# Pooled attention with a SoLU feed-forward on one core: the second product of a tile one slot later

## The chip, the cores and the metric

The kernel runs on one core of one Trainium2 chip. The metric is device time in microseconds, the median of several executions. TensorE appears as PE (matmuls) and PEld (weight loads), VectorE as DVE, ScalarE as ACT, GpSimd as POOL, and the queue from which SyncE issues DMAs as SP or SPq.

## What is computed

Four batches of 12288 queries with 128 channels attend to 768 pooled keys each, and the result goes through a feed-forward block with a softmax-weighted activation and a layer norm:

```
kv_flat = mean over 4x4 patches of kv, reshaped, @ w_sr      # keys = values, 768 x 128
s = (q @ k.T) / sqrt(128);  a = softmax(s);  x = a @ v
h = x @ w_in                                                  # 1024 wide
u = h * softmax(h)
ln = (u - mean(u)) / sqrt(var(u) + 1e-6) * g_ln
out = ln @ w_out                                              # 128 wide
```

## The kernel before

There are 384 tiles (`NT`) of 128 tokens, 96 per batch, four to a group (`GT`), 96 groups (`NG`). Products are made in split precision: an operand is a 16-bit high part plus a 16-bit low part, and a product is three matmul passes. The order of all instructions is written out by hand (`manual_schedule`): each engine works through its instructions in exactly the order in which the source emits them, and the only other order is that of the waits between engines for data and for buffers.

The main loop (line 1056) runs over 384 slots. In one slot the engines work on several tiles, each at another stage. Counted from the slot of its scores, a tile passes these stages; a name with a line number is the instruction as the trace shows it:

- Slot 0: DVE takes the negated row maximum of the scores (`nm`, L575), ACT the exponential (`s`, L576) and its 16-bit high part (`phl`, L578), DVE the low part (`phl`, L586), and SP transposes both by DMA (`pT`, L589). The scores themselves (PE, `s`, L555) were made one slot earlier.
- Slots 2 to 6 of the last tile of a group, for the whole group: PE makes `xa` (L622), ACT and DVE split it (`xh` L629, `xl` L634), DVE takes a reciprocal (`rz`, L657).
- Slot 9: PE makes `h` (L675). Slot 10 (`LH`): DVE takes its maximum (`junkd`, L683), ACT the exponential (`e`, L699).
- Slot 11: DVE makes `u` (L713), POOL its high part (L730) and low part (L737) in `uhl`, ACT the sum of squares (`junk`, L778), and `hidden_turn` (line 750) issues the DMA that transposes `uhl` into `uT` (L752). `uT` has 4 buffers (line 746).
- Slot 13 (`LO`, line 44): `final_pe` (line 788) makes `o`, the second product of the block: 24 matmuls of 128 columns that read `uT` (L803).
- Per group: `final_scale` (ACT, `f`, L813) and `final_root` (POOL, L820 and L821) make the norm factor; `final_out` (line 823) is called at `slot - LO - 1` of the last tile of a group: it multiplies on DVE (`ob`, L826) and issues the store to HBM on SP (L835).

`final_out` runs once per group, so it falls in a fixed one of every four slots. With the slot number taken modulo four, the extra work per group lies so: in slots 3 ACT has `f` and SP the load of queries (`qf`, L503); in slots 0 ACT has `xh`, and SP, where keys of the next batch are due, a load of 384 KB (`kv`, L229); in slots 1 DVE has `xl` early and `rz` late, ACT `rz` (L662) and the high part of the next queries (`qh`, L533). In the kernel before, `ob` and its store are in slots 1, behind `rz`, too. Slots 2 have nothing extra.

PSUM holds three 2-bank buffers that scores and `h` share (`ps_r`), one bank for `xa` and one for `o` (`ps_o`). So `h` of a slot waits for the DVE `phl` of that slot to release a buffer, and the first `o` of a group waits for `ob` of the group before it.

Keys of batch 0 are made before the loop and used in a wider format, which makes its slots longer on PE. Those of batches 1 to 3 are loaded and added up in slots up to 62, 64 to 156 and 160 to 252 (one load in 6 slots) and turned into `kh`, `kl` and `vhl` in slots 69 to 92 of the batch before (165 to 188 and 261 to 284 for batches 2 and 3).

After the loop a list of calls (`tail`, line 1160) finishes the last ten tiles. In it `("o", -4)` is the second product of tile `NT - LH - 4`, and so on. The last slot of the loop makes no `o` (line 1107).

Of the kernel before, what the change touches and what calls it, by code (L numbers as in the profile page):

```python
# [40 lines left out]
XSP = 5  # L41
NORM = 6
LH = 10
LO = 13
FSC = 12
QSP = 1

# [20 lines left out]
def kernel(  # L68
# [429 lines left out]
    def q_load(g):  # L498
        if g >= NG or g % QL:
            return  # L500
        b, gb = divmod(g, GPB)
        t = dmt.tile([P, QL * 512], F32, tag="qf", name=f"qf_{g}", bufs=3)
        nc.sync.dma_start(t, qT[b, :, gb * 512 : (gb + QL) * 512])  # L503
        state["qf", g // QL] = t
# [121 lines left out]
    def values_out(g):  # L626
        b = g * GT // TPB
        xh = grp.tile([P, 512], F16, tag="xh", name=f"xh_{g}")
        nc.scalar.activation(xh, state["xa", g], AF.Copy, scale=state["sv", b][:, 1:2])  # L629
        state["x", g] = (xh, grp.tile([P, 512], F16, tag="xl", name=f"xl_{g}"))  # L630
# [12 lines left out]
    def values_norm(g):  # L643
        b = g * GT // TPB
        zz = grp.tile([P, 2, GT], F32, tag="zz", name=f"zz_{g}", bufs=2)
        rz = grp.tile([P, 3, GT], F32, tag="rz", name=f"rz_{g}", bufs=3)
        z, bb = state.pop(("z", g)), state["bb", b]
        for k in range(2):
            nc.gpsimd.tensor_scalar(
                zz[:, k, :], z, 1e-9, bb[:, 3 + k : 4 + k], op0=ALU.add, op1=ALU.mult  # L650
            )
        state["zz", g] = (zz, rz)
# [383 lines left out]
    def at(t, fn, *args):  # L1036
        if 0 <= t < NT:
            fn(t, *args)

    def at_last(t, fn, *args):  # L1040

        if 0 <= t < NT and t % GT == GT - 1:
            fn(t // GT, *args)
# [12 lines left out]
    for slot in range(NT):  # L1056
# [50 lines left out]
        if slot < NT - 1:  # L1107
            at(slot - LO, final_pe)
        if late:
            values(av, qtr, 1)  # L1110
        at(i - 1, hidden_turn)
        if slot % GT == GT - 1:
            q_load(slot // GT + 3)
        at_last(slot - LO - 1, final_out)
        at_last(slot - XSP, values_out)
# [44 lines left out]
    def tail(steps):  # L1160
        for name, *ts in steps:
            fn = {
                "h": hidden_pe, "o": final_pe, "max": hidden_max, "e": hidden_exp,
                "u": hidden_u, "hl": split, "sq": hidden_var,
                "t": hidden_turn_pe, "th": hidden_turned_high, "tl": hidden_turned_low,
            }[name]
            for t in ts:
                fn(NT - LH + t)
# [1 line left out]
    xa(G - 1, 3)  # L1170
    values_norm(G - 1)
    values_norm(G)
    tail([("h", 1), ("u", -1)])
    values_out(G - 1)
    tail([("max", 0), ("e", 0), ("hl", -1)])
    scale(G - 1)
# [129 lines left out]
```

## Time and profile before

| | |
|---|---|
| median of 3 runs | 1850.34 us (1846.69 to 1851.47) |
| the profiled execution | 1846.07 us, span 1844.2 us |
| busy: PE, PEld | 1819.9 us (99%), 1187.9 us (64%) |
| busy: ACT, DVE, POOL | 1781.8 (97%), 1768.6 (96%), 1684.9 (91%) |
| PE, ACT, DVE busy in 560 to 700 us | 136.43, 135.49, 134.61 of 140 |
| PE, ACT, DVE busy in 1500 to 1640 us | 140.00, 139.02, 137.89 of 140 |
| DMA busy share, bytes per time | 1.19 and 235 GB/s in 560 to 700 us, 1.18 and 227 GB/s in 1500 to 1640 us |
| TensorE clock granted | 0.999 of the upper level |
| DMA issues | `pT` x384, 4.1 us to landing; `uT` x378, 4.5 us |

Shares of busy time are averages over stretches with different limits. PE's row counts a matmul until its modelled end, which lies after the start of the next one, so a PE at 100% may still start its matmuls late; waits and start-to-start times say more. The share of the DMA engines counts the packets of 16 engines and can be over 1 since an engine has more than one packet under way.

### The profile page before, as it was taken

Reading aid. Unit: us, or ns where it says so; the run is one execution under the profiler, and the core shown is the slowest. Engines: PE = TensorE matmul, PEld = TensorE weight load, DVE = VectorE, ACT = ScalarE, POOL = GpSimd, SP = SyncE. Lnnn points to the kernel's source line nnn. Section 1 sums busy time; section 2 is a strip of 40 time slices with the busy share of each in tenths; the row PEclk is TensorE's granted clock in tenths of the full one; section 3 lists DMA queues with packets and bytes.
Section 4 is the critical chain, followed back from the end, with each engine's and each line's share of the span. In section 5 each row is a group of like instructions: output and inputs, shape, how many; then the busy total and the mean of one; then the engine's idle time right before and its main releaser. Section 6 shows DMA issues by size and latency. Waiting matters only on the chain.

```text
span 1844.2 us, 42743 instructions
## 1 busy us (share of the span) xinstructions
PE 1819.9 (99%) x15723; PEld 1187.9 (64%) x15723; DVE 1768.6 (96%) x2635; ACT 1781.8 (97%) x3124; POOL 1684.9 (91%) x1466
## 2 busy tenths in 40 slices
PE   8999999999999999999999999999999999999998
PEld 5567777777666666666666666666666666666666
DVE  6999999999999999999999999999999999999997
ACT  5999999999999999999999999999999999999997
POOL 5899999899999999989999999998998989898987
PEclk9999999999999999999999999999999999999999
DMA  8999999999999999999999999999999999999998
GB/s 301 211 221 241 233 242 238 237 235 239 240 240 231 239 238 246 246 235 235 236 238 243 240 242 241 240 242 226 222 233 233 232 229 229 228 230 238 227 211 176
DMA packets 1440027, 432.80 MB, mean 235 GB/s; under 512 B 1404608, under 2 KB 1408832, under 8 KB 1439552
## 3 DMA queue, kind: packets, MB, share of 16 engines
q1 hardware_dynamic: 1439664, 429.97, 115.3%
q8 instruction: 126, 2.06, 0.5%
q14 instruction: 93, 0.76, 0.1%
q10 hardware_dynamic: 144, 0.00, 0.0%
HBM read 52.50 MB, written 25.17 MB: 42 GB/s over the span
## 4 chain that ended last, share of the span: by engine, by line
ACT 44%; PE 32%; POOL 9%; issue 7%; DMA 3%; DVE 3%; SPq 0%; POOLq 0%; DVEq 0%
ACT e L699 12%; ACT junk L778 12%; PE o L803 9%; ACT phl L578 9%; PE h L675 8%; PE s L555 7%; ACT s L576 7%; PE xa L622 7%; POOL uhl L737 4%; ACT qh L533 2%; POOL uhl L730 2%; DMA uT<-uhl 2%; DMA kv<-in_kv_dram 1%; DVE junkd L683 1%; ACT xh L629 1%
## 5 line engine op out<-in xcount | busy, mean ns | idle before, releaser
L737 POOL TENSOR_TENSOR uhl<-u,uhl 128x1024 f16<-128x1024 f32 x382 | 814.9, 2134 | 31.6
L803 PEld LDWEIGHTS <-uT 128*128 128x128 f16 x9072 | 537.0, 98 | 97.6 <-DMA uT<-uhl 11.8
L803 PE MATMUL o<-wch,uT 128*128 128x128 f16 x6048 | 568.2, 219 | 5.9 <-DMA uT<-uhl 5.8
L803 PE MATMUL o<-wcl,uT 128*128 128x128 f16 x3024 | 525.9, 219 | 0.0
L713 DVE SCALAR_TENSOR_TENSOR u<-h,rz,e 128x1024 f32<-128x1024 f32 x384 | 491.0, 1279 | 29.7 <-ACT e L699 22.8
L683 DVE TENSOR_SCALAR_CACHE_REDUCE junkd<-h,rz 128x1024 bf16<-128x1024 f32 x384 | 490.5, 1277 | 1.5 <-PE h L675 1.1
L622 PE MATMUL xa<-pT,vhl 128*128 128x512 f16 x1728 | 468.9, 380 | 0.0
L699 ACT ACTIVATE e<-h,nm,rz 128x1024 f32<-128x1024 f32 x384 | 458.5, 1194 | 3.0 <-DVE junkd L683 3.0
L730 POOL TENSOR_SCALAR uhl<-u 128x1024 f16<-128x1024 f32 x379 | 397.0, 1047 | 66.3 <-DVE u L713 57.8
L778 ACT ACTIVATE junk<-u,su 128x1024 bf16<-128x1024 f32 x384 | 437.4, 1139 | 0.1
L575 DVE TENSOR_REDUCE nm<-s 128x1 f32<-128x768 f32 x384 | 363.8, 947 | 15.5 <-PE s L555 14.6
L586 DVE SCALAR_TENSOR_TENSOR phl<-s,phl 128x768 f16<-128x768 f32 x384 | 365.6, 952 | 5.0 <-ACT phl L578 4.9
L576 ACT ACTIVATE s<-s,nm 128x768 f32<-128x768 f32 x384 | 335.0, 872 | 6.3 <-DVE nm L575 5.9
L578 ACT ACTIVATE phl<-s 128x768 f16<-128x768 f32 x384 | 311.5, 811 | 12.1
L675 PEld LDWEIGHTS <-xh 128*128 128x128 f16 x1536 | 140.4, 97 | 197.5 <-DVE phl L586 39.1
L622 PEld LDWEIGHTS <-vhl 128*128 128x128 f16 x1728 | 162.1, 98 | 140.8 <-issue 13.1
L675 PE MATMUL h<-w_in_h,xh 128*128 128x512 f16 x768 | 229.1, 380 | 2.9 <-DVE rz L657 1.8
L675 PE MATMUL h<-w_in_h,xl 128*128 128x512 f16 x768 | 228.4, 379 | 0.0
L675 PE MATMUL h<-w_in_l,xh 128*128 128x512 f16 x768 | 228.4, 379 | 0.0
L555 PEld LDWEIGHTS <-qh 128*128 128x128 f16 x1152 | 108.0, 98 | 56.5 <-issue 0.6
L555 PE MATMUL s<-kh,qh 128*128 128x384 f16 x576 | 140.5, 325 | 0.4 <-DVE u L713 0.3
L555 PE MATMUL s<-kh,ql 128*128 128x384 f16 x576 | 140.7, 326 | 0.0
(150 smaller groups left out, 1856.1 us busy)
## 6 DMA issues: line engine op xcount, KB each, us to landing
kv<-in_kv_dram SPq DMA_DIRECT2D x64, 384.0 KB, 4.5
qf<-in_q_dram SPq DMA_DIRECT2D x96, 256.0 KB, 3.3
out_dram<-ob SPq DMA_DIRECT2D x96, 256.0 KB, 2.7
pT<-phl SPq DMA_TRANSPOSE x384, 4.1
uT<-uhl SPq DMA_TRANSPOSE x378, 4.5
raw_in<-in_moe_w_in_dram SPq DMA_DIRECT2D x1, 1024.0 KB, 5.2
raw_out<-in_moe_w_out_dram SPq DMA_DIRECT2D x1, 1024.0 KB, 9.6
room<-uhl SPq DMA_TRANSPOSE x5, 3.7
```

Of the source, the lines that this page charges most:

```text
L555: nc.tensor.matmul(s[:, half, :384], lh[:, ts], rh[:, half * 384 : (half + 1) * 384], start=n == 0, stop=n == 2,)
L576: nc.scalar.activation(s, s, AF.Exp, bias=nm, accum_out=state["z", g][:, j : j + 1])
L578: nc.scalar.mul(phl[:, 0], s, SC)
L622: nc.tensor.matmul(xa, v[:, c, :], pT[:, :, a * NKC + c, :], start=n == 0, stop=n == len(seq) - 1)
L675: nc.tensor.matmul(h[:, hs], lh[:, ts], rh[:, hs], start=n == 0, stop=n == 2)
L683: nc.vector.tensor_scalar(junk, state["h", t], state["rz", g][1][:, j : j + 1], None, op0=ALU.mult, op1=ALU.min, accum_out=nm,)
L699: nc.scalar.activation(e, state["h", t], AF.Exp, bias=nm, scale=state["rz", g][0][:, js], accum_out=state["z2", g][:, js],)
L713: nc.vector.scalar_tensor_tensor(u, state.pop(("h", t)), state["rz", g][2][:, j : j + 1], state.pop(("e", t)), op0=ALU.mult, op1=ALU.mult, ...
L730: nc.gpsimd.tensor_scalar(uhl[:, 0, :], u, 1.0, 1.0, op0=ALU.mult, op1=ALU.mult)
L737: low.tensor_tensor(uhl[:, 1, :], u, uhl[:, 0, :], op=ALU.subtract)
L778: nc.scalar.activation(junk, u, AF.Square, scale=-float(DFF), bias=su, accum_out=state["v3", g][:, j : j + 1],)
L803: nc.tensor.matmul(po[:, ts], uT[:, a * NFC + c, :], w[:, c, :], start=start, stop=stop)
```

## The change

`LO` goes from 13 to 14, so `final_pe` of a tile is emitted one slot later, and with it `final_out` of a group, which moves from slots 1 to slots 2 (modulo four). `uT` keeps its 4 buffers. The loop then ends one `o` earlier, and the list after the loop makes that one (tile 369) first:

```
-LO = 13
+LO = 14
...
-    tail([("h", 1), ("u", -1)])
+    tail([("h", 1), ("o", -5), ("u", -1)])
```

`final_scale` and `final_root` keep their slots (`FSC` is unchanged), and so do all other stages.

## Rows read from the trace of the kernel before

**Rows 1.** The page's first part: busy time, share of the span, instructions of each engine

```profile
PE 1819.9 (99%) x15723; PEld 1187.9 (64%) x15723; DVE 1768.6 (96%) x2635; ACT 1781.8 (97%) x3124; POOL 1684.9 (91%) x1466
```

**Rows 2.** The list of waits: who waited for whom: us, times, longest

```profile
PEld L803 <- DMA uT<-uhl: 11.8, 14, 1.7
...
ACT s L576 <- DVE nm L575: 5.9, 13, 1.0
PE o L803 <- DMA uT<-uhl: 5.8, 10, 1.2
```

**Rows 3.** Timeline of ACT, slots 1 to 3: start, us, instruction

```profile
1513.04 1.20 ACT L699 ACTIVATE e<-h,nm,rz 128x1024 f32<-128x1024 f32 x1
...
1514.23 0.28 ACT L662 ACTIVATE rz<-rz,bb 128x4 f32<-128x4 f32 x1
1514.42 1.11 ACT L533 CAST qh<-qf 128x512 f16<-128x512 f32 x1
1515.49 0.88 ACT L576 ACTIVATE s<-s,nm 128x768 f32<-128x768 f32 x1
...
1516.52 0.81 ACT L578 ACTIVATE phl<-s 128x768 f16<-128x768 f32 x1
...
1518.36 1.20 ACT L699 ACTIVATE e<-h,nm,rz 128x1024 f32<-128x1024 f32 x1
...
1519.63 0.88 ACT L576 ACTIVATE s<-s,nm 128x768 f32<-128x768 f32 x1
...
1538.02 0.88 ACT L576 ACTIVATE s<-s,nm 128x768 f32<-128x768 f32 x1
```

**Rows 4.** Timeline of DVE, the same slots

```profile
1513.89 0.70 DVE L826 SCALAR_TENSOR_TENSOR ob<-o,swi,f 128x512 f32<-128x512 f32 x1
1514.51 0.95 DVE L575 TENSOR_REDUCE nm<-s 128x1 f32<-128x768 f32 x1
1515.37 1.27 DVE L713 SCALAR_TENSOR_TENSOR u<-h,rz,e 128x1024 f32<-128x1024 f32 x1
...
1516.58 1.28 DVE L683 TENSOR_SCALAR_CACHE_REDUCE junkd<-h,rz 128x1024 bf16<-128x1024 f32 x1
...
1517.78 0.95 DVE L586 SCALAR_TENSOR_TENSOR phl<-s,phl 128x768 f16<-128x768 f32 x1
1518.65 0.94 DVE L575 TENSOR_REDUCE nm<-s 128x1 f32<-128x768 f32 x1
```

**Rows 5.** Timeline of PEld, slots 127 to 129, with the wait before in brackets

```profile
611.55 1.34 PEld L803 LDWEIGHTS <-uT 128*128 128x128 f16 x24 [1.54 <-DMA uT<-uhl]
...
618.20 0.91 PEld L622 LDWEIGHTS <-vhl 128*128 128x128 f16 x5
```

**Rows 6.** Timeline of the SP queue: the transposes that rows 5 need

```profile
605.06 4.33 SPq L752 DMA_TRANSPOSE uT<-uhl  x1
...
613.33 1.53 SPq L589 DMA_TRANSPOSE pT<-phl  x1
```

**Rows 7.** Timeline of PEld: the second product of a tile near slot 374

```profile
1758.88 1.54 PEld L803 LDWEIGHTS <-uT 128*128 128x128 f16 x24
```

**Rows 8.** Timeline of the SP queue: a transpose three tiles after rows 7

```profile
1763.68 1.75 SPq L752 DMA_TRANSPOSE uT<-uhl  x1
```

**Rows 9.** Timeline of ACT, slots 1 and 2 where keys are prepared

```profile
807.12 1.15 ACT L533 CAST qh<-qf 128x512 f16<-128x512 f32 x1
808.14 0.90 ACT L576 ACTIVATE s<-s,nm 128x768 f32<-128x768 f32 x1
...
809.19 0.81 ACT L578 ACTIVATE phl<-s 128x768 f16<-128x768 f32 x1
```

**Rows 10.** Timeline of DVE, the same slot 2

```profile
810.03 0.96 DVE L586 SCALAR_TENSOR_TENSOR phl<-s,phl 128x768 f16<-128x768 f32 x1 [0.68 <-ACT phl L578]
```

**Rows 11.** Timeline of ACT, slot 382, where no `qh` follows `rz`

```profile
1791.26 0.88 ACT L576 ACTIVATE s<-s,nm 128x768 f32<-128x768 f32 x1 [0.98 <-DVE nm L575]
```

**Rows 12.** Timeline of PEld: `h` of slot 14, just after the first second product

```profile
75.72 0.55 PEld L675 LDWEIGHTS <-xh 128*128 128x128 f16 x4 [0.40 <-DVE phl L586]
```

## The prediction

> **What bounds the kernel now.** I read the page's first part, then the list of waits, then the timelines of single slots. In the first part all five engines are over nine tenths busy [rows 1], so a saving on one of them is worth only what the next one leaves. The list of waits names what the change aims at: PE and its weight loads wait for the DMA of uT [rows 2]. The row of PE has 10 such waits with 5.8 us; it ends a matmul 0.16 after the start of the next one, so from start to start these ten cost 5.8 + 10 x 0.16 = 7.4 us. Nine lie in the loop (6.9 us), one in the tail (0.5). Two lie in batch 0 (0.8 and 0.4 us, slots 27 and 68), four in slots 124 to 142 (together 4.2) and three in slots 220 to 226 (1.6), all while keys are loaded. [rows 5] show one in slot 127. From slot 289 on there is none.
>
> There the timelines say what sets the pace. ACT repeats a group of four slots in 1538.02 - 1519.63 = 18.39 us [rows 3], 4.60 a slot. Slots are numbered modulo four from here on, and s(3) is the exp in a slot 3. DVE runs from ob to nm(3) without a gap [rows 4], and s(2) and s(3) each start 0.98 us after the start of their nm [rows 3, 4], which is when nm is done: PE, ACT and DVE are tied, and ACT waits a little for DVE twice a group.
>
> **The change part by part.** (1) The o waits. Each tile's o comes one slot (4.6 us) later against its transposition. The longest wait listed is 1.7 us [rows 2], so all nine go, 6.9 us at most. At least the two in batch 0 are real gain (1.1), since no other wait follows them closely.
>
> (2) The buffers. The transposition of tile t+4 must wait until o(t) has read its buffer; were it late, SP would wait, and behind it the next pT, the loads and the store, and PE for those. In place of o(t) its slot will hold what is now o(t+1). Near the end, where SP is least behind, that block ends at 1758.88 + 1.5 = 1760.4 and the transposition three tiles later is issued at 1763.68 [rows 7, 8]: 3.3 us to spare. Were the margin gone, each microsecond of it would cost one. Cost 0.
>
> (3) ob moves on DVE from the end of slot 1 to the end of slot 2. Its 0.62 us (1513.89 to 1514.51) [rows 4] now stand right before nm(2), while ACT has qh to do, 1.07 us. In slot 2 it will stand between phl(2) and nm(3), where ACT has no extra work. DVE gets ahead by 0.62 in slot 2 first, but phl(2) can't start before ACT's phl: where DVE waited for it, it started 810.03 - 809.19 = 0.84 after that one's start [rows 9, 10]. So from the start of ACT's phl(2) to s(3): 0.84, then phl 0.87 (1517.78 to 1518.65), ob 0.62, nm to s 0.98 = 3.31. Today it is 1519.63 - 1516.52 = 3.11 [rows 3]. ACT itself needs 3.03: 1518.36 - 1516.52 = 1.84 until e starts, and 1.19 for e (1513.04 to 1514.23). ACT's wait grows from 0.08 to 0.28, +0.20 a group. Back comes a little at s(2), for which nm will be early: qh takes 1.02 where nothing is waited for (807.12 to 808.14) [rows 9] instead of 1.07: -0.05. Since ACT's order is a closed ring, its group becomes 18.39 + 0.15 = 18.54 us.
>
> (4) Where that counts. In batch 0 PE is longer than ACT and hides it. In slots 97 to 381 there are 71 groups: 23 from slot 289 on (23 x 0.15 = 3.4), 30 while keys are loaded (4.5) and 18 while keys are prepared. In the last, ACT, DVE and POOL have extra work of uneven size; between nothing and 2.7, I take 2.0, since in rows 9 and 10 phl(2) waits for ACT, and the whole 0.3 would follow. Together 9.9, between 7.9 (nothing there) and 14.2 (0.20 in all 71).
>
> (5) The store of ob moves on SP past one pT and one uT; those two go out 0.5 to 0.8 us earlier, and the store lands in front of the next pT. The loads of slots 3 and 0 and the store no longer follow each other in three slots. SP had no gap between these rows [rows 6], so the sum is the same: 0. The bank of o is released by ob: o moves by a slot, 4.6 us, and ob from 1513.89 to about 1516.52 + 0.84 + 0.87 = 1518.2, by 4.3, so the bank is free a little earlier than now against the o that needs it: 0. POOL's order doesn't change.
>
> (6) Ends. The first slot with o loses it, but h of the next slot waits for DVE 0.40 anyway [rows 12]: gain 0 to 0.1. In the list after the loop one o more, 24 weight loads in 1.34 [rows 5], stands between h(1) and the next o on a PE without gaps; the end hangs on POOL and a DMA as well, and the chain of work that ended last runs through those, not through PE, for most of the tail. Cost 0 to 1.34, I take 0.7. In slot 382 ACT waits 0.98 for an nm behind ob [rows 11]; this goes, but nm(3) follows, inside the same bounds.
>
> Sum against the profiled execution: 1846.07 - 6.9 + 9.9 + 0.7 = 1849.8 us, +3.7. The three timed runs lie at 1846.7 and 1850 to 1851; the profiled one is at the low end. I set the sum on the mean of all four, 1848.6: 1852.3, rounded to **1852**.
>
> **The rivals.** *A, the loop with ob doesn't bind.* If ACT's wait is taken up by slack I don't see, only (1) and (6) are left: -6.2, 1842.4 on the mean of the four. For it: PE is fullest [rows 1], and its matmuls have no slack of their own. Against: s starts exactly 0.98 after nm in slots 2 and 3. 15%.
>
> *B, DMA takes back its part.* In slots 120 to 130 SP issues one transposition behind the other. pT of slot 127 is issued at 613.33 [rows 6], with 4.1 us to landing at 617.4, and PE needs it at 618.20 [rows 5]: 0.8 us to spare, by the estimate. If PE runs 2.5 us ahead after two waits are gone, it waits there instead. Then (1) gives 1.1 in batch 0, about 0.8 to 1.2 in each of the two stretches, 3.1 in all: 1852.3 + 3.8 = 1856. Against it: part (3) slows the same stretches by 0.15 a group, which gives DMA time. 15%.
> The Trainium skill, Perfetto Trace Analysis, "What 'DMA-bound' means", says that an issuing sequencer whose track is solid DMA slices can itself be the bound; by that rule this rival holds wherever SP's track is solid, as it is here in 605 to 615 us.
>
> *C, slower: ACT's wait in full.* Place: s(3) behind ob. If s(2) gives nothing back, it is 0.20 in all 71 groups, 14.2; with half of the o waits gained (3.5) and 1.3 at the end it is +12.0, 1860.6. If phl(2) didn't move up at all, the wait would be 0.62 and the price 44 us; rows 4 speak against that, since DVE has no gap between ob and phl(2). To pass +0.3% it takes 0.19 a group with 6.9 gained, or 0.14 with 3.5. 25%.
> The Trainium skill, Perfetto Trace Analysis, "Identifying the Most-Contended Engine", doesn't count matmul busy time as nearness to the limit but the flops done and the share of weight loads, here 64%, and takes the engine with the highest occupancy otherwise, here ACT. By that rule waits on PE cost nothing and waits on ACT all: this rival, without its gain. Against it, the o waits show up as longer slots (four of them make slots 121 to 145 slower by 4.2 us than their neighbours).
>
> **How the numbers follow.** Forecast 45%, 1848 to 1856 by its bounds (part 4 at 7.9 to 10.6 and the tail at 0 to 1.3, with 2 us for the runs). 0.3%, 5.5 us, is about what a measurement can tell from no change: faster is below 1844.8, slower above 1855.9. A falls mostly under faster (12 of 15), B on both sides of the upper bound (8 of 15 under the same), C under slower (23 of 25), the forecast under the same (all but 1). That gives faster 0.12, same 0.57 (3 of A, 8 of B, 2 of C, 44 of the forecast), slower 0.31 (7 + 23 + 1). The range reaches toward A and C: 1843.5 to 1860, which leaves out about 2 in 10.
>
> **What would show it.** In the profile after: no wait of o for uT in the loop; ob after phl in slots 2; ACT s waiting for nm in slots 3 by 0.25 to 0.3 us, some 60 to 70 waits with 15 to 20 us in place of 13 with 5.9; ACT's group at 18.5 us from slot 289 on; POOL's and SP's rows as they are. I am wrong if groups there still take 18.39 (A), if PE waits for pT in slots 124 to 145 (B), or if they take 18.6 and more (C).

## The result, and the profile after

| | before | after |
|---|---|---|
| median | 1849.8 us | 1861.2 us (1858.6 to 1865.0) |
| ratio | | 1.0061, 95% interval 1.0048 to 1.0073 |
| the profiled execution | 1846.07 us, span 1844.2 | 1860.6 us, span 1858.8 |

The change costs 11.4 us by the medians, 14.5 by the two profiled executions: that of the kernel before lies 3.7 us under its median, that of the changed kernel 0.6 under its own. The forecast was 1852, with a range up to 1860. The first part of the page after, beside [rows 1], shows little: PE is busy 8 us longer in a span that is 14.6 us longer.

```profile
PE 1827.8 (98%) x15723; PEld 1184.6 (64%) x15723; DVE 1768.2 (95%) x2635; ACT 1779.9 (96%) x3124; POOL 1684.9 (91%) x1466
```

The list of waits after (who waited for whom: us, times, longest) says more when it is read against [rows 2]:

```profile
ACT s L576 <- DVE nm L575: 28.0, 97, 1.1
DVE phl L586 <- ACT phl L578: 13.1, 24, 1.0
...
PE xa L622 <- DMA pT<-phl: 7.6, 8, 2.0
...
PEld L622 <- DMA pT<-phl: 6.6, 6, 2.4
```

The o waits on uT have left the list. Two things have come: ACT waits for `nm` 97 times in place of 13, and PE waits for pT, which it never did before. The second is about as long as the wait that went (7.6 us here, 5.8 in [rows 2]).

Where the time went is best seen by stretches. The table gives the length of stretches of slots, from the starts of `s` on ACT, in one profiled execution each; a stretch is from the `s` of its first slot to that of its last.

| slots | what is in it | before | after | difference |
|---|---|---|---|---|
| up to 1 | start | 32.2 | 32.7 | +0.5 |
| 1 to 97 | batch 0 | 433.8 | 435.4 | +1.6 |
| 97 to 121 | loads | 110.3 | 111.4 | +1.1 |
| 121 to 145 | loads, four o waits before | 114.4 | 113.3 | -1.1 |
| 145 to 157 | loads | 55.1 | 57.4 | +2.2 |
| 157 to 205 | keys prepared, loads | 226.1 | 227.3 | +1.1 |
| 205 to 229 | loads, three o waits before | 111.9 | 111.4 | -0.5 |
| 229 to 241 | loads | 55.1 | 57.5 | +2.4 |
| 241 to 289 | loads, keys prepared | 224.1 | 226.3 | +2.2 |
| 289 to 381 | no loads | 422.9 | 427.0 | +4.2 |
| behind 381, to the end of the last `ob` | list after the loop | 52.9 | 53.6 | +0.7 |

There is a steady growth of about 0.18 us a group, seen bare from slot 289 on (427.0 / 23 = 18.57 against 18.385). With that taken off, the stretches with o waits gain 2.2 and 1.6 us, and the stretch right behind each of them loses 1.7 and 1.8.

The steady part, in the timelines of DVE and then ACT, slot 2 into slot 3, beside [rows 3, 4]:

```profile
1526.95 1.28 DVE L683 TENSOR_SCALAR_CACHE_REDUCE junkd<-h,rz 128x1024 bf16<-128x1024 f32 x1
...
1528.32 0.96 DVE L586 SCALAR_TENSOR_TENSOR phl<-s,phl 128x768 f16<-128x768 f32 x1
1529.20 0.74 DVE L826 SCALAR_TENSOR_TENSOR ob<-o,swi,f 128x512 f32<-128x512 f32 x1
1529.86 0.95 DVE L575 TENSOR_REDUCE nm<-s 128x1 f32<-128x768 f32 x1
```

```profile
1512.28 0.88 ACT L576 ACTIVATE s<-s,nm 128x768 f32<-128x768 f32 x1 [0.23 <-DVE nm L575]
...
1527.48 0.81 ACT L578 ACTIVATE phl<-s 128x768 f16<-128x768 f32 x1
...
1530.84 0.88 ACT L576 ACTIVATE s<-s,nm 128x768 f32<-128x768 f32 x1 [0.23 <-DVE nm L575]
```

It is the chain of the prediction, row for row: `phl` on DVE 0.84 behind ACT's (1528.32 - 1527.48), `ob` behind it, `nm`, and `s` 0.98 behind the start of `nm`. `s` of slot 3 waits 0.23 us each time, and the group takes 1530.84 - 1512.28 = 18.56 us.

The other part, at the longest new wait of PE: the rows of the SP queue, then the row of PE.

```profile
726.19 1.73 SPq L752 DMA_TRANSPOSE uT<-uhl  x1
728.02 0.53 SPq L835 DMA_DIRECT2D out_dram<-ob  x1
728.64 1.51 SPq L589 DMA_TRANSPOSE pT<-phl  x1
730.26 3.80 SPq L752 DMA_TRANSPOSE uT<-uhl  x1
```

```profile
734.65 1.25 PE L622 MATMUL xa<-pT,vhl 128*128 128x512 f16 x5 [2.00 <-DMA pT<-phl]
```

The store now stands right in front of the last pT of its group (slot 151). That pT is issued at 728.64, it lands at 734.60, and PE can start `xa` at 734.65, 6.0 us after the issue.

### The profile page after: what moved, and what is told of

Its sections match the earlier page's. It is cut to its first block, busy times and chain, and to the rows that moved or that the text cites. A ratio compares the mean times of both kernels' runs of the same rounds, so it can differ in the third digit from the quotient of the medians.

```text
span 1858.8 us, 42676 instructions
## 1 busy us (share of the span) xinstructions
PE 1827.8 (98%) x15723; PEld 1184.6 (64%) x15723; DVE 1768.2 (95%) x2635; ACT 1779.9 (96%) x3124; POOL 1684.9 (91%) x1466
## 4 chain that ended last, share of the span: by engine, by line
ACT 50%; PE 25%; DVE 11%; issue 9%; DMA 3%; POOL 1%; SPq 0%; DVEq 0%; ACTq 0%; POOLq 0%
ACT e L699 12%; ACT junk L778 11%; ACT phl L578 11%; ACT s L576 10%; PE o L803 7%; PE h L675 7%; PE xa L622 6%; PE s L555 5%; DVE nm L575 4%; DVE phl L586 3%; DVE ob L826 2%; DMA pT<-phl 2%; DVE junkd L683 1%; ACT qh L533 1%; ACT xh L629 1%
## 5 line engine op out<-in xcount | busy, mean ns | idle before, releaser
L713 DVE SCALAR_TENSOR_TENSOR u<-h,rz,e 128x1024 f32<-128x1024 f32 x384 | 490.4, 1277 | 32.2 <-ACT e L699 32.0
L578 ACT ACTIVATE phl<-s 128x768 f16<-128x768 f32 x384 | 311.1, 810 | 12.3 <-DMA pT<-phl 0.2
L622 PEld LDWEIGHTS <-vhl 128*128 128x128 f16 x1728 | 161.3, 98 | 151.9 <-issue 18.6
L555 PE MATMUL s<-kl,qh 128*128 128x384 f16 x576 | 140.7, 326 | 0.0
(150 smaller groups left out, 1861.2 us busy)
```

Source lines behind the costliest of these rows:

```text
L555: nc.tensor.matmul(s[:, half, :384], lh[:, ts], rh[:, half * 384 : (half + 1) * 384], start=n == 0, stop=n == 2,)
L578: nc.scalar.mul(phl[:, 0], s, SC)
L622: nc.tensor.matmul(xa, v[:, c, :], pT[:, :, a * NKC + c, :], start=n == 0, stop=n == len(seq) - 1)
L713: nc.vector.scalar_tensor_tensor(u, state.pop(("h", t)), state["rz", g][2][:, j : j + 1], state.pop(("e", t)), op0=ALU.mult, op1=ALU.mult, ...
```

## Experiments

Three theories were set against each other. Ring: `ob` between phl(2) and nm(3) makes the chain through ACT and DVE longer. Queue: while keys are loaded, SP and the transfers behind it are full, so waits only move from uT to pT. Store: the store's new place on SP makes the transfers late.

### Each term by itself

Kernel 1, only `ob` moved back out of the chain, the store left where the change put it:

```
+        at_last(slot - LO - 1, lambda g: final_out(g, later=True))
         if slot >= LH:
             at(slot, scores_split)
...
-        at_last(slot - LO - 1, final_out)
+        at_last(slot - LO - 1, final_store)
```

> The changed kernel with ob taken in front of phl(2) on DVE instead of behind it; the store keeps its place. Ring theory (the extra 0.18 us a group comes from ob between phl(2) and nm(3)): DVE then fills the 0.13 us in which it waits for ACT's phl(2), s(3) waits 0.1 us or less in place of 0.23, groups from slot 289 on take 18.40 to 18.45 us in place of 18.57, and some 71 to 90 groups x 0.13 = 9 to 12 us come back: 1849 to 1852. Queue theory (the time goes to pT waits in the stretches with loads, whatever DVE does): groups from 289 on may fall, but the load stretches stay at their length, so at most 71 - 30 = 41 groups x 0.13 = 5 us come back: 1856. If the place of ob does not matter: 1861.

Measured: 1857.7 us, ratio to the kernel before 1.0041 (1.0025 to 1.0057). DVE and ACT in a slot 2, from the timelines:

```profile
1523.91 0.74 DVE L826 SCALAR_TENSOR_TENSOR ob<-o,swi,f 128x512 f32<-128x512 f32 x1
1524.58 0.95 DVE L586 SCALAR_TENSOR_TENSOR phl<-s,phl 128x768 f16<-128x768 f32 x1
1525.44 0.95 DVE L575 TENSOR_REDUCE nm<-s 128x1 f32<-128x768 f32 x1
```

```profile
1523.25 0.81 ACT L578 ACTIVATE phl<-s 128x768 f16<-128x768 f32 x1
...
1526.42 0.88 ACT L576 ACTIVATE s<-s,nm 128x768 f32<-128x768 f32 x1
```

`s` follows phl(2) after 3.17 us in place of 1530.84 - 1527.48 = 3.36, and groups from slot 289 on take 18.385 us, the time of the kernel before to the last digit. The ring is shown. But only 3.5 of the 9 to 12 us came back, because the load stretches got longer: slots 121 to 157 took 173.1 us (169.5 before, 170.7 after), and the pT waits of PEld grew from 6.6 to 11.0 us, while those of PE fell from 7.6 to 4.3.

Kernel 2, only the store moved back on SP, `ob` left in the chain:

```
-        at_last(slot - LO - 1, final_out)
+        at_last(slot - LO - 1, lambda g: final_out(g, later=True))
+        at_last(slot - LO - 4, final_store)
```

> The changed kernel with only the store of ob issued three slots later on SP, in a slot 1, where it stood before; ob itself stays between phl(2) and nm(3). Store theory (the store now stands in front of the last pT of a group and makes it late): the eight waits of PE on pT (7.6 us, some 8 to 9 from start to start) go, 1852 to 1854. Queue theory (SP and DMA are full in those stretches, whatever the order): pT waits of 5 us or more stay, 1859 to 1862. Ring theory alone: no change, 1861, groups from 289 on still 18.57 us.

Measured: 1855.0 us, 1.0030 (1.0021 to 1.0040), 6.2 below the changed kernel. Its list of waits has no row of PE for a DMA of the loop any more; the ring's row is about as it was:

```profile
ACT s L576 <- DVE nm L575: 24.6, 96, 0.8
```

Groups from slot 289 on take 18.57 us. So the store's place has a price of its own.

Kernels 3 and 4, the changed kernel and the kernel before without 42 of the loads of kv:

```
+        if pos > 1:
+            state["kv", b, pos] = state["kv", b, 1]
+            return
         t = dmt.tile([P, 2, 384], F32, tag="kvc", ...)
```

> The changed kernel without 14 of the 16 loads of kv for each of the batches 1 to 3 (the sums add the second load again instead; so part of the input is left out and the output differs). POOL's and PE's instructions are the same. Queue theory: the pT waits go; slots 145 to 157 and 229 to 241 fall from 57.4 us to about 55.7, slots 49 to 61 by 1 us; in all 6 to 9 us, 1852 to 1855. Store theory: the pT waits stay, 1861. Ring theory alone: groups from 289 on at 18.57 us, no change.

> The kernel before without the same 42 loads (again part of the input is left out). Queue theory: the o waits on uT go without moving o, some 6 to 7 us, 1842 to 1844; then the changed kernel with the same loads left out stands 10 to 14 us above this one, which is the ring's share (about 70 groups x 0.15 to 0.18) and the tail's 0.7. If the o waits come from the transpositions alone, they stay: 1849.

The kernel has a general second pass behind the loop, which it takes when a sum is out of range; with the other sums it takes it, so the totals (7379 and 7361 us) say nothing of the loop; its rows do.

| slots 1 to 381, one execution each | with the loads | without | the loads' share |
|---|---|---|---|
| before | 1753.7 | 1747.1 | 6.6 |
| after | 1767.0 | 1760.4 | 6.6 |
| difference | +13.3 | +13.3 | 0.0 |

Before, the loads cost 6.6 us through o waits; after, they cost 6.6 us through pT waits; in these executions nothing of that was gained. Without the loads all that differs in the loop is the ring, 13.3 us, which is 0.7 in batch 0, 8.3 in slots 97 to 289 and 4.3 behind them. Two things limit this reading. It rests on one execution of each kernel, and by the medians the change costs 3 us less than by these executions; if that scatter lies in the stretches with loads, some 3 us of the o waits were gained after all. And kernel 2, which has the slow ring and the store in its old place, takes 1760.5 us in the same slots with all the loads, the 1760.4 that the changed kernel takes without them: there the o waits are a gain in full. So the 6.6 us of the changed kernel are the price of the store's place, and that they equal the o waits is chance.

### Is it the store or the late o?

Kernel 6, the kernel before with nothing but the store one slot later on SP:

```
-        at_last(slot - LO - 1, final_out)
+        at_last(slot - LO - 1, lambda g: final_out(g, later=True))
+        at_last(slot - LO - 2, final_store)
```

> The kernel before (o 13 slots behind) with one edit: the store of ob is issued one slot later on SP, in a slot 2, as in the changed kernel; ob and o stay. Store theory: PE waits on pT appear in slots 120 to 157 and 217 to 241, 4 to 8 us in all, while groups from slot 289 on stay at 18.385: 1853 to 1857 beside 1850. If the store's place matters only together with the late o (PE then runs ahead in the load stretches): no more than 1 us, 1850.

Measured: 1857.5 us, 1.0042 (1.0024 to 1.0059), 8.8 above the kernel before, groups from 289 on at 18.389. The price was as the store theory has it, the place was not: the list of waits has those of `o` on uT, and next to none on pT (PE 0.8 us, PEld 0.8).

```profile
PEld L803 <- DMA uT<-uhl: 31.3, 36, 2.3
...
PE o L803 <- DMA uT<-uhl: 15.2, 20, 1.8
```

With `o` 13 slots behind, uT has the least slack, and it shows the delay; with 14, pT has. Which row waits depends on the slack of its reader, and how late the queue is depends on the queue.

Kernel 5, both parts moved (`ob` as in kernel 1, the store as in kernel 2):

> The changed kernel with both parts moved: ob in front of phl(2) and the store three slots later on SP, in a slot 1. If the change is three terms that add (o waits gone -6.6, ring +13.3, store's place +6.5), two of them are gone: groups from slot 289 on at 18.385 us, no PE wait on pT or uT in the loop, slots 1 to 381 in 1747 us as with the loads left out, and in all 6 us below the kernel before, about 1844 beside 1850. If a faster DVE order brings the pT waits back whatever the store's place (queue theory, as they grew when only ob was moved), slots 145 to 157 and 229 to 241 stay 2 us or more above 55.2 and it is about 1849 to 1851.

Measured: 1846.3 us, 0.9985 (0.9976 to 0.9995). Against kernel 1 the store's place is worth 11.4 us. It is 2.5 us below the kernel before, not 6: groups are at 18.385, but PE waits 4.7 us for pT again, most of it in slots 121 to 157 (168.8 us) and 205 to 241 (169.3). Kernel 2, with the same store and the slower ring, has none of these waits: a faster loop leaves the queue less time, as the queue theory said. So the two edits don't add: alone they bring 3.5 and 6.2 us, together 14.9.

What the queue does there is seen in SP's rows. In slots 121 to 157 the changed kernel issues 96 DMAs; they take 160.2 us, and between two of them lie 0.094 us, 9.0 in all: together 169.2 of 169.2 us. SP is never idle there, in any kernel that has the loads. Without the loads it issues for 145.0 us and idles for 21.6. Six loads have 6 x 0.57 = 3.4 us of issue of their own, so the other 12 us are transpositions whose issue got shorter; the reading is that an issue lasts longer while the transfers ahead of it move. Solid rows alone make nobody wait: in kernel 2 they are as solid (159.1 us of issue and 9.1 between, in 168.2), and PE waits for none of them (PEld once, for 0.2 us).
The Trainium skill, Perfetto Trace Analysis, "What 'DMA-bound' means", names a solid issuing track among the things that can bind a kernel; kernel 5 agrees with its 4.7 us of pT waits, kernel 2 doesn't. It also says that such slices are the making of descriptors and not the movement of data; these 12 us speak against that here, and the measurement decides.

### Where in the ring

Kernel 7, `ob` behind nm(3), the store in a slot 1:

```
         at(slot, scores_exp)
+        at_last(slot - LO - 2, lambda g: final_out(g, later=True))
```

> The changed kernel with the store in a slot 1 and ob behind nm(3), in front of u(3). Ring theory, by the durations: with ob out of the way nm(3) is done some 0.33 us before ACT wants it, but then ob 0.66, u 1.20, junkd 1.20, phl 0.88 and nm 0.98 stand between nm(3) and s(0), 4.8 us behind the end of nm(3), while ACT needs 4.32 from s(3) to s(0): s(0) waits some 0.15 us a group in place of s(3), groups from slot 289 on take 18.45 to 18.55 us, some 1851 to 1855. If only the place between phl(2) and nm(3) is bad: 18.385 and about 1844.

Measured: 1849.9 us (1844.6 to 1858.6), ratio 1.0000 (0.9985 to 1.0014), groups from 289 on at 18.388 us. ACT and DVE from slot 3 into slot 0:

```profile
1513.01 0.87 ACT L576 ACTIVATE s<-s,nm 128x768 f32<-128x768 f32 x1
...
1517.49 0.88 ACT L576 ACTIVATE s<-s,nm 128x768 f32<-128x768 f32 x1
```

```profile
1512.57 0.74 DVE L826 SCALAR_TENSOR_TENSOR ob<-o,swi,f 128x512 f32<-128x512 f32 x1
...
1515.63 0.95 DVE L586 SCALAR_TENSOR_TENSOR phl<-s,phl 128x768 f16<-128x768 f32 x1
1516.50 0.95 DVE L575 TENSOR_REDUCE nm<-s 128x1 f32<-128x768 f32 x1
```

The wait came where it was expected: s(3) to s(0) is 4.48 in place of 4.33. The group did not get longer. (The whole kernel is 3.6 us above kernel 5, with intervals that overlap; its stretches with loads are longer, and why stays open.) The time from one `s` to the next, by slot class (medians over slots 296 to 371), says why:

| from s of slot | 0 | 1 | 2 | 3 | sum |
|---|---|---|---|---|---|
| before | 4.604 | 5.316 | 4.139 | 4.326 | 18.385 |
| after | 4.601 | 5.265 | 4.379 | 4.324 | 18.569 |
| kernel 1 | 4.602 | 5.267 | 4.194 | 4.325 | 18.388 |
| kernel 7 | 4.613 | 5.250 | 4.045 | 4.475 | 18.383 |
| least of each column | 4.601 | 5.250 | 4.045 | 4.324 | 18.220 |

Three different orders give the same 18.385, so ACT's ring doesn't set it. PE does: in 1420 to 1680 us it is busy all 260.00 us in the kernel before and in kernels 1 and 7, and 259.68 in the changed one. The rows of before, of after and of kernel 1, with the columns window, length, busy time (instructions) of PE, PEld, DVE, ACT and POOL, granted clock, DMA share, GB/s:

```profile
1420.00:1680.00 260.00, 260.00 (x2287) 165.51 (x2284) 256.31 (x384) 258.23 (x455) 233.64 (x205) 1.00 1.18 230
```

```profile
1420.00:1680.00 260.00, 259.68 (x2273) 162.98 (x2271) 253.73 (x379) 254.98 (x449) 231.62 (x203) 1.00 1.16 227
```

```profile
1420.00:1680.00 260.00, 260.00 (x2300) 165.77 (x2298) 256.11 (x382) 257.50 (x454) 233.84 (x206) 1.00 1.17 230
```

These sums hide most of what the changed kernel loses on PE (0.32 us of 14 x 0.18 = 2.5), since a matmul counts as busy until its modelled end. The starts show it. In the changed kernel five `xa` are followed by `h` after 1525.04 - 1523.78 = 1.26 us in one slot of a group, where that `h` waits for DVE, and after 1.08 in the next:

```profile
1523.78 1.24 PE L622 MATMUL xa<-pT,vhl 128*128 128x512 f16 x5
1525.04 0.59 PE L675 MATMUL h<-w_in_h,xh 128*128 128x512 f16 x2
...
1528.65 1.24 PE L622 MATMUL xa<-pT,vhl 128*128 128x512 f16 x5
1529.73 0.59 PE L675 MATMUL h<-w_in_h,xh 128*128 128x512 f16 x2
```

Summed over slots 293 to 373, the matmuls of the kernel before and of kernels 1 and 7 start 0.05 us a group later than back to back (the median distance of a line taken as back to back, delays under 0.015 us left out), and those of the changed kernel 0.23. The difference is the 0.18 of the ring.

By an estimate from the table, ACT alone would need 18.22 us (the least of each column), so it has 0.165 us a group to give away under PE. Behind nm(3) `ob` costs 0.15 of that, and the group pays nothing; between phl(2) and nm(3) it costs 4.379 - 4.045 = 0.33, and 0.18 shows.

### Where on the queue

In kernels 9 and 10 `ob` stands in front of phl(2) as in kernel 5, and the store is issued in a slot 3 (the edit shown) and in a slot 0 (`- 3` in place of `- 2`):

```
-        at_last(slot - LO - 4, final_store)
+        at_last(slot - LO - 2, final_store)
```

> As the kernel with both parts moved (ob in front of phl(2)), but the store stands in a slot 3 on SP, right behind the load of q, and so behind the last pT of its group. If a store in front of pT(3) is what costs (place theory): like the store in a slot 1, 1845 to 1848. If a store is cheap only where it stood, because two transfers in a row hold up the transpositions behind them: 1853 or more, with SP's issue time in slots 121 to 157 above 162 us in place of 159.4.

> The same with the store in a slot 0, in front of the load of kv where there is one. Place theory (only a store in front of pT(3) costs): 1845 to 1848. Two transfers in a row: 1853 or more, SP's issue time in slots 121 to 157 above 162 us.

Measured: 1872.2 us in a slot 3 (1.0122, 1.0108 to 1.0137), 1846.2 in a slot 0 (0.9989, 0.9978 to 0.9999). Both theories fell: in a slot 3 the store is behind pT(3) and costs most, in a slot 0 it stands in a row with the load of kv and costs nothing. The SP rows of kernel 9 show the next pT held up. Behind the load of q it takes 2.6 us on the mean of slots 121 to 157, and 1.5 in kernel 5; the uT below is longer than most (2.3 on the mean, 2.8 in kernel 5):

```profile
705.05 0.57 SPq L503 DMA_DIRECT2D qf<-in_q_dram  x1
705.67 0.42 SPq L841 DMA_DIRECT2D out_dram<-ob  x1
706.21 2.53 SPq L589 DMA_TRANSPOSE pT<-phl  x1
708.83 3.81 SPq L752 DMA_TRANSPOSE uT<-uhl  x1
```

Over slots 121 to 157 the issues took 168.0 us there, 159.4 in kernel 5, 159.3 in kernel 10.

Kernel 12 leaves the store in the bad slot 2 (it is kernel 1) and moves the load of q away from it, one slot later; kernel 13 brings the load of q near the store of kernel 5 (there the condition is `slot % GT == 2 and slot > 2`, which is also three slots later for each group):

```
-        if slot % GT == GT - 1:
-            q_load(slot // GT + 3)
+        if slot % GT == 0 and slot:
+            q_load(slot // GT + 2)
```

> The changed kernel with ob in front of phl(2) and the store in a slot 2, as measured at 1857.7, with one more edit: the load of q is issued one slot later, in a slot 0 in place of a slot 3, so it stands two slots behind the store and beside the load of kv. Neighbour theory (a store costs where the load of q is one slot or less away): 1845 to 1849, SP's issue time in slots 121 to 157 at 159 to 160 us in place of 161.9. Place theory (a store in a slot 2 holds up pT(3), whatever else is loaded): 1855 to 1859.

> The kernel with both parts moved (store in a slot 1, measured at 1846.3), with the load of q issued one slot earlier in its cycle, in a slot 2, so it stands one slot behind the store, as in the changed kernel. Neighbour theory: 1853 to 1859. Place theory: 1845 to 1849.

Measured: kernel 12 1845.4 us (0.9973, 0.9961 to 0.9985), 12.3 below kernel 1. So a store in a slot 2 is not dear in itself. Kernel 13 took 1849.3 (1.0001, 0.9988 to 1.0014), 3 us above kernel 5, less than the neighbour theory wanted, and its list of waits has a new one, since q now comes too late for POOL:

```profile
POOL qf L519 <- DMA qf<-in_q_dram: 10.0, 11, 2.7
```

PE's waits for pT are 8.4 us there against 4.7 in kernel 5, as the neighbour theory would have, but with the new wait beside them the run decides nothing. What can be said is that the store is dear in a slot 2 or 3 while the load of q is in a slot 3, and cheap in the other orders tried, with kernel 13 open.

Kernels 14 and 15 are the kernel before and the changed kernel with that load of q alone in a slot 0:

> The kernel before (o 13 slots behind, ob and store in a slot 1) with only the load of q issued one slot later, in a slot 0 beside the load of kv. If the gain of the fastest kernel (1845.4) comes from o standing a slot later, this one stays at 1848 to 1851. If it comes from the load of q, it is at 1844 to 1847.

> The changed kernel with only the load of q issued one slot later, in a slot 0. The store's term (6.2 us, 1861.2 against 1855.0) goes if its price hangs on the load of q: 1854 to 1857, groups from slot 289 on still 18.57 us since the ring is as it was. If the store in a slot 2 costs by itself: 1860 to 1862.

Measured: 1847.7 us (0.9987, 0.9975 to 0.9998) and 1854.9 (1.0028, 1.0019 to 1.0037). One edit, which moves the load of q, takes from the changed kernel the same 6 us as moving the store did, and leaves the ring. In the kernel before it is worth 2. The fastest kernel is kernel 12; its interval overlaps that of kernel 14, so whether the late `o` brings something by itself is not settled.

Kernel 11, kernel 5 with the loop's stores issued by POOL:

```
-        nc.sync.dma_start(rows..., ob...)
+        (nc.gpsimd if to is None and g < 92 else nc.sync).dma_start(rows..., ob...)
```

> As the kernel with both parts moved, but the stores of the loop are issued by POOL's queue in place of SP's. In slots 121 to 157 SP issues without a gap in every kernel with the loads (159 to 164 us of issue and 96 x 0.094 between them). If the number of issues on SP is the limit, SP loses 9 x 0.66 = 6 us in those 36 slots, the pT waits go and it is 1840 to 1843. If the transfer behind the queue is the limit (a transposition is issued when there is room), the issues of the transpositions get longer by as much and it stays at 1845 to 1848. If POOL's own time for the issue counts (POOL is 0.9 busy), groups from slot 289 on rise above 18.385.

Measured: 1875.4 us (1.0144, 1.0130 to 1.0159), a time that none of the three had; the third had the cause, POOL's own time, but looked for it from slot 289 on. The pT waits went, and POOL became the limit where keys are loaded. Its timeline has the issue as an instruction:

```profile
609.86 2.13 POOL L737 TENSOR_TENSOR uhl<-u,uhl 128x1024 f16<-128x1024 f32 x1
611.94 0.63 POOL L841 DMA_DIRECT2D out_dram<-ob  x1
612.60 1.01 POOL L240 TENSOR_TENSOR ka<-ka,kv 128x384 f32<-128x384 f32 x1
```

In slots 205 to 229 groups take 114.0 / 6 = 19.0 us, 0.61 over 18.385, which is the 0.63 of that row: with the sums of kv POOL has no room left. From 289 on, without them, groups take 18.385. SP's rows stayed solid as well: 87 issues took 160.2 us in slots 121 to 157, where 96 took 159.4.
The Trainium skill, DMA: Bandwidth & Descriptors, "Issuing engines are not separate DMA queues", says that issuing from several engines saves only the time of the issue, since the transfers share the same engines; SP's 160.2 us are in line with it, in slots that POOL made longer (170.9 us against 168.8).

### The list after the loop

Kernel 8 is kernel 5 with the added `o` behind h(2) and in front of the `o` of tile -3:

```
-    tail([("h", 1), ("o", -5), ("u", -1)])
+    tail([("h", 1), ("u", -1)])
...
-    ... ("hl", 0), ("o", -3)])
+    ... ("hl", 0), ("o", -5), ("o", -3)])
```

> As the kernel with both parts moved, and in the list after the loop the added o stands behind h(2) and the o after it instead of in front of them. If the added o holds up h(2) there (its share is at most 1.34 us, and the stretch behind slot 381 took 0.7 us more than before), 0.5 to 1 us comes back, 1843 to 1843.5. If POOL and the DMA set the tail, no change against the kernel with both parts moved.

Measured: 1846.3 us, the same as kernel 5, and the stretch behind slot 381 is 53.7 us in both. This doesn't clear the added `o`. PE works through that list without a gap. In the changed kernel h(2) starts 18.38 us behind `s` of slot 381, in place of 17.13 before. In kernel 8 it starts at 17.14, but now two `o` stand in front of h(3), which starts at 21.11 in place of 19.76. Either way one `h` and all behind it come 1.25 to 1.35 us later, and of that 0.7 to 0.8 is left at the last `ob`.

## Why the prediction was wrong

(1) The o waits. All nine went, as forecast, and their size was right (6.6 us by the kernels without loads, 6.9 by the rows). With the store in its old place and the ring as in the changed kernel this was a gain in full (kernel 2: 1760.5 us in the loop with the loads, 1760.4 without). In the changed kernel as much came back as waits for pT. That is the sign of rival B, at 15%, but B's reason, that SP issues one transposition behind the other, is not enough for it, since SP's rows are as solid in kernel 2. Where the loop is faster, with ring and store both put right (kernel 5), 2.5 us were left.

(2) The buffers of uT. Cost nothing, as forecast: the transposition four tiles on, which takes the same buffer, was issued at least 2.8 us after `o` had read it.

(3) `ob` on DVE. Right in mechanism and place, small in size: 3.36 from phl(2) to s(3) against 3.31, since `ob` takes 0.66 before the next instruction there and not 0.62; s(2) came 0.05 earlier as forecast. 18.57 a group against 18.54. The ground under it was wrong: the prediction read a loop set by ACT with 0.08 of wait, and it is PE that sets 18.385 ([rows 3, 4] are as true of a ring that follows PE). That the size came out so near is in part luck: 0.33 on ACT less 0.165 of slack gives about what 0.20 less 0.05 does.

(4) Where it counts. 13.3 us in the loop, of which 4.3 behind slot 289 (forecast 3.4), 8.3 in slots 97 to 289 (6.5) and 0.7 in batch 0 (0). Most groups of batch 0 take 18.73 us in both kernels and hide the ring, as forecast; the 0.7 comes in slots 73 to 81, where keys are prepared. Inside the bounds of 7.9 to 14.2, at their upper end: the second term that was mis-sized, by 3.4 us.

(5) The store. The step that failed outright: "the sum is the same: 0". It counted what is in the queue and not the order in it, though [rows 6] had the sign: one uT took 4.33 us to issue and one pT 1.53. The runs price the place at 6.2 us (changed kernel against kernel 2), 8.8 (kernel 6 against before) and 11.4 (kernel 1 against kernel 5). Moving the load of q in place of the store takes off 6.3 us (kernel 15). Why this order is dear stays open.

(6) The ends. 0.7 us, as forecast, and by the forecast's way: one more `o` on a PE without gaps puts h(2) 1.25 us later, and of that 0.7 is left at the end.

So the forecast's -6.9 + 9.9 + 0.7 should have read -6.6 + 13.3 + 0.7 and 6.5 for the store's place (1767.0 - 1760.5): 13.9 us, and 14.4 with the 0.5 by which this execution started later, where 14.5 were measured. By its time rival C came out (1860.6), but that is luck: it gave 14.2 for the ring, kept half of the o waits and had no price for the store. Of what would show the forecast, the chain was there, and so were the waits of ACT (70 in slots 3 from 97 to 381, with 18.7 us; the other 27 of the list lie in batch 0 and in the last two slots); groups took 18.57, nearer to the 18.6 of C. The sign of rival B, PE waiting for pT in slots 124 to 157, was there too. One reading of [rows 1] was wrong without harm: four rows are over nine tenths, not five, since PEld is at 64%.

## What to carry to other kernels

A wait on a transfer that is removed is a gain only if the next reader of the same queue doesn't then wait in its place. Solid rows of the issuing queue warn of that, but don't decide it: with solid rows the o waits were a gain in full in kernel 2, in part in kernel 5, and in the changed kernel as much came back. Before costing an instruction that moves on an engine, find out which engine sets the group's time and how much each of the others has to give away beneath it, slot by slot; the same 0.66 us on DVE cost 0, 0 and 0.18 us a group in three places, in groups without loads. The order of loads and stores among transpositions is a term of its own: try it, since here one edit that moves a load was worth 6 us.

## What was unexpected of the hardware

- The order of DMAs on a full queue changed the time that their issues took: 156.4 to 168.0 us for the same 96 DMAs in slots 121 to 157, by where the store and the load of q stood. As the rows are solid, their sum follows the length of the slots too, so the small values needn't be the least that the queue could do. The reason is open. It doesn't follow from the store's distance to the last pT, from two plain transfers in a row, or (so far as kernel 13 shows) from closeness to the load of q alone.
- In the stretches with loads the kernels that differ in nothing that such a stretch sees still scatter in one execution: 168.8 and 169.9 us in slots 121 to 157 for kernels 5 and 8. Medians were needed there, while groups without loads repeat to 0.005 us.
- A store issued by POOL costs POOL 0.63 us as an instruction.
